# Wider instructions in an attention stage: two heads' maxima and scores per two-bank tile, rows scaled in one instruction, float64 conversion in 28 pieces

## The chip, the cores and the metric

The kernel runs on one NeuronCore of a Trainium2 chip. TensorE (PE) multiplies, VectorE (DVE) and ScalarE (ACT) do elementwise work, GpSimd (POOL) helps, and SyncE (SP) issues nearly all DMAs. The metric is the device time in microseconds (us), and the median of several executions is compared.

## The reference, cut to what matters

Three parts run one after the other; the output of each is the input of the next.

```python
# q, k, v: (4, 12, 448, 64) float32
q_n, k_n = rmsnorm(q, g_q), rmsnorm(k, g_k)
scores = scale * np.matmul(q_n, k_n.transpose(0, 1, 3, 2))
scores = scores - np.max(scores, axis=-1, keepdims=True)
attn = np.exp(scores)
attn = attn / (np.sum(attn, axis=-1, keepdims=True) + 1e-09)
out = np.matmul(attn, v)
# mixture of experts: 1792 tokens, 8 experts of at most 224 tokens, greedy assignment
h = np.maximum(x[mask] @ w1[e], 0.0);  out[mask] = h @ w2[e]
# cos MLP
h = x @ w_in;  return (h * np.cos(h)) @ w_out
```

`w_in` (768x2048) and `w_out` (2048x768) arrive as float64. The kernel reads them as pairs of 32-bit words and turns each number into a float32 high and low half before the last part uses them.

## The kernel before, in words

**The order of work.** No engine's order is written by hand. Each operation is recorded as a step (`Plan.add`, through the helper at line 47, which is why most rows of the profile carry L47), with what it reads and writes. `Plan.run` then places the steps one by one with a fixed cost for each (`Plan.cost`) and a due time worked out backwards from the end; on each engine, the step that can start first goes first, and among those about equally early the one due first. Each engine's instructions are issued in that order, and semaphores do the rest. There are two plans: `attention` (with the first part of the routing and the conversion), then `moe` (routing, experts, MLP). All instructions of the first plan stand ahead of those of the second on each engine.

**Attention** works on 24 pairs of heads (4 batches x 6 pairs). For a pair, `turn` scales the rows and transposes them with PE into `kk` and `qq`. `shifts` finds for every query the maximum of its scores: seven products `s` of 448 columns go one after the other through a ring of two PSUM tiles (`b1`, tile name `s1`, one bank each), and DVE reduces each into a column of `cm`. Three products belong to each head, on 64 of PE's rows, and the seventh is shared. The maxima are transposed, negated by ACT into `cr`, and copied by two small DMAs (`sr<-cr`) into one row. `scores` makes, for each of four blocks of 112 keys, the two heads' scores with eight matmuls of 64 rows each (the last two add the negated maxima from `sr`), into the two PSUM tiles of ring `bs` (`st`), one head in each; ACT takes the exponential of each into a tile `pf`. `weigh` multiplies `pf` with the values (`po`) and sums the rows (`dn`). `rows` and `tail` transpose the result and scale it: DVE writes `xk` in two halves of 256 columns; for the last pair ACT does it in eight pieces.

**Conversion.** `Narrow` works through 56 pieces (32 of `w_in`, three blocks of 128 rows each; 24 of `w_out`, four blocks each; `EARLY = 56` puts all of them into the attention plan). A piece is loaded into `nr` (a ring of four), ACT takes magnitudes into `na`, DVE does two `tensor_scalar`, two `scalar_tensor_tensor` and, after another ACT step, one `tensor_tensor`, and a DMA stores the piece to DRAM. These steps depend on no step of attention; they share its engines. In `moe`, `narrow.plan` is called once more with nothing left to do, and only allocates tiles.

Of the kernel before, what the change touches and what calls it, by code (L numbers as in the profile page):

```python
# [15 lines left out]
I32 = mybir.dt.int32  # L16
AF = mybir.ActivationFunctionType
ALU = mybir.AluOpType
AX = mybir.AxisListType
# [31 lines left out]
class Plan:  # L51
# [96 lines left out]
    def ring(self, pool):  # L148

        def make(name, n, shape, dt=F32):  # L150
            tiles = [pool.tile(shape, dt, name=f"{name}{i}") for i in range(n)]
            at = [0]

            def take():
                at[0] += 1
                return tiles[(at[0] - 1) % n]
            return take
        return make
# [93 lines left out]
class Narrow:  # L252
# [1 line left out]

    WIDE = {"wi": 3, "wo": 4}

    def __init__(self, nc, pairs):

# [11 lines left out]
    def plan(self, plan, pool, last):  # L272

        nc = self.nc
        most = max(self.WIDE.values())
        raw = [pool.tile([128, most, 256], I32, name=f"nr{b}") for b in range(4 - (self.i > 0))]
        mag = [pool.tile([128, most, 128], I32, name=f"na{b}") for b in range(2)]
        v = plan.vector
        for i, (src, dst, name) in enumerate(self.todo[self.i:last]):
            n = dst.shape[1]  # L280
            r, a = raw[i % len(raw)][:, 0:n], mag[i % 2][:, 0:n]
            words, o = r.rearrange("p k (n t) -> p k n t", t=2), r.bitcast(F32R).rearrange("p k (h n) -> p k h n", h=2)
            low, high, f = words[:, :, :, 0], words[:, :, :, 1], a.bitcast(F32)
            plan.add([("SP", 0.46, lambda r=r, src=src: nc.sync.dma_start(r, src))], [], [r], dma=0.36 * n)
            plan.scalar.activation(f, high.bitcast(F32), AF.Abs)
            v.tensor_scalar(f, f, LEAST, MOST, op0=ALU.max, op1=ALU.min)
            v.tensor_scalar(a, a, 3, 0x3FFFFFF8, op0=ALU.logical_shift_left, op1=ALU.bitwise_and)
            v.scalar_tensor_tensor(a, high, -0x40000000, a, op0=ALU.bitwise_and, op1=ALU.bitwise_or)
            v.scalar_tensor_tensor(a, low, 29, a, op0=ALU.logical_shift_right, op1=ALU.bitwise_or)
            plan.scalar.activation(o[:, :, 0], f, AF.Copy)  # L290
            plan.either("tensor_tensor", o[:, :, 1], f, o[:, :, 0].bitcast(F32), op=ALU.subtract)
            plan.add([("SP", 0.46, lambda o=o, dst=dst: nc.sync.dma_start(dst, o.bitcast(F32)))], [o], [name], dma=0.36 * n)
        self.i = last


B, H, S, D = 4, 12, 448, 64
CP, NC = 112, 4
# [4 lines left out]
EPS = 1e-9  # L302
SAME = 4.0
TUNE_A = (3.5, 0.3, 4.5, 0.7, 30.0, 1.2)
NPF = 18
NXE = 6
LAST = 3
COLD = 20
# [3 lines left out]
ACC = ()  # L312
END = 20.0
NKQ = 5
XKA = 0
XKL = 1
QND = False
SSA = 1
# [17 lines left out]
def attention(tc, P, R, ident, q, k, v, g_q, g_k, w_gate, x_dram, L, other):  # L336
# [4 lines left out]
    with ExitStack() as ctx:  # L341
        cst = ctx.enter_context(tc.tile_pool(name="a_cst", bufs=1))
        pp = ctx.enter_context(tc.tile_pool(name="a_ps", bufs=1, space=PSUM))
        ve, sc, pe = P.vector, P.scalar, P.tensor
        ring = P.ring(cst)

        def bank(name, n):
            return P.ring(pp)(name, n, [128, 512])

        keys = [cst.tile([128, 2, S], F32R, name=f"kk{i}") for i in range(NKQ)]  # L350
        queries = [cst.tile([128, 2, S], F32R, name=f"qq{i}") for i in range(NKQ)]
# [5 lines left out]
        ones = cst.tile([CP + 1, 2, 32], F32, name="ones")  # L357
        part = cst.tile([CP, NC, 8, H + 1], F32, name="part")
        raw = ring("qk", 3, [CP, 2, 4, NC * D])
# [6 lines left out]
        mix = [cst.tile([128, 128], F32R, name=f"mx{i}") for i in range(4)]  # L366
        cms = ring("cm", 2, [128, 2 * NC])
        crs = ring("cr", 2, [2 * NC, 128], F32R)
        pfs = ring("pf", NPF, [CP + 1, S])
        xes = ring("xe", NXE, [128, S])  # L370
        dns = ring("dn", 2, [128, CP])
        xks = ring("xk", 2, [CP, NC, 2 * UP * D])
        recs = ring("r", 3, [CP, NC, 2])
        abs_ = ring("ab", 1, [CP, 2, NC, 128], BF16)
        NPR = B * NP
        bt, b1, bs, bo, bd = bank("t", 2), bank("s1", 2), bank("st", 2), bank("po", 1), bank("dn", 1)

        R.on(P, bd)

# [34 lines left out]
        for i, g in enumerate((g_q, g_k)):  # L414
            for z in range(2):
                o = gcol[z * D:(z + 1) * D, i:i + 1]
# [64 lines left out]
        def shifts(P_):  # L481


            cm, x = cms(), 7
            k, q = keys[P_ % NKQ], queries[P_ % NKQ]
            for m in (0, 4, 1, 5, 2, 6, 3):
                p = b1()[:, :S]
                if m == 3:
                    w, y = mix[P_ % 4], k[:, 0]
                else:  # L490
                    h, c = (0, 128 * m) if m < 3 else (1, D + 128 * (m - 4))
                    r = slice(h * D, (h + 1) * D)
                    w, y = q[r, 0, c:c + 128], k[r, 0]
                pe.matmul(p, w, y, start=True, stop=True)
                ve.tensor_reduce(cm[:, m:m + 1], p, AX.X, ALU.max)
            p, cr = bt()[0:x, 0:128], crs()[0:x]
            pe.transpose(p, cm[:, 0:x], ident)
            sc.activation(cr, p, AF.Copy, scale=-1.0)
            t = shift_rows[P_ % 4]
            for h in range(2):  # L500
                copy(t[h * D:h * D + 1].rearrange("o (m p) -> o m p", p=128), cr[3 * h:3 * h + 4])
# [17 lines left out]
        def scores(P_, a, z):  # L519

            k, q, t = keys[P_ % NKQ], queries[P_ % NKQ], shift_rows[P_ % 4]
            for c in range(a, z):
                sl = slice(c * CP, (c + 1) * CP)
                ps = [bs()[0:CP, :S] for h in range(2)]

                def both():
                    for j in range(4):
                        for h in range(2):
                            r = slice(h * D, (h + 1) * D)
                            w = heads[r] if j == 3 else k[r, j == 1, sl]  # L530
                            y = t[r, h * D:h * D + S] if j == 3 else q[r, int(j == 2)]
                            pe.matmul(ps[h], w, y, start=j == 0, stop=j == 3)

                P.halves = True
                block(both)
                P.halves = False
                for h in range(2):
                    pf = exps[P_, h, c] = pfs()
                    sc.activation(pf[0:CP], ps[h], AF.Exp)

        outs = {}

        def weigh(P_):


            po, pd = bo()[:, :S], bd()[:, 0:CP]
            t = vals.pop(P_).rearrange("p h (c d) -> p h c d", d=D)
            P.beside = True
            for c0 in range(0, NC, 2):
                def both():  # L550
                    for c in range(c0, c0 + 2):
                        for h in range(2):
                            pe.matmul(po[h * D:(h + 1) * D], t[:, h, c], exps[P_, h, c][0:CP], start=c == 0,
                                      stop=c == NC - 1)

                block(both)
            sums_of[P_] = pd
            outs[P_] = xes()
            sc.activation(outs[P_], po, AF.Copy)

            def sums():
                for h in range(2):
                    for c in range(NC):
                        n, e = CP + (c == 0), exps.pop((P_, h, c))
                        for j in range(NC):
                            pe.matmul(pd[32 * j:32 * j + 32], ones[0:n, h], e[0:n, j * CP:(j + 1) * CP],
                                      start=h == 0 and c == 0, stop=False)

            block(sums)

            def logits():
                for j in range(NC):
                    pe.matmul(pd[32 * j:32 * j + 32], wg[:, P_ % NP], outs[P_][:, j * CP:(j + 1) * CP], start=False,
                              stop=True)

            block(logits)
            P.beside = False
# [16 lines left out]
        def tail(P_, xk, e, r):  # L594
            xe, p = outs.pop(P_), bt()[0:CP]
            P.begin()
            for c in range(NC):
                pe.transpose(p[:, c * 128:(c + 1) * 128], xe[:, c * CP:(c + 1) * CP], ident)
            P.finish()
            for z in range(2):  # L600
                cs = slice(2 * z, 2 * z + 2)
                o = xk[:, cs, 2 * e * D:2 * (e + 1) * D].rearrange("p c (h d) -> p c h d", h=2)
                i = p.rearrange("p (c h d) -> p c h d", c=NC, h=2)[:, cs]
                if z < XKA or P_ >= NPR - XKL:
                    for c in range(2):
                        for h in range(2):
                            sc.activation(o[:, c, h], i[:, c, h], AF.Copy, scale=r[:, 2 * z + c, h:h + 1])
                else:
                    ve.tensor_tensor(o, i, r[:, cs].unsqueeze(3).to_broadcast([CP, 2, 2, D]), op=ALU.mult)

        roots_of, xk_of = {}, {}

# [80 lines left out]
CP, NCOL, E, CAP = 112, 16, 8, 224  # L693
# [415 lines left out]
def moe(tc, P, R, ident, x_rows, w1, w2, w_in, w_out, out, narrow):  # L1109

    nc = tc.nc
    with ExitStack() as ctx:
# [172 lines left out]
            nc.gpsimd.memset(apart, 0.0)  # L1285

        P.shared = False
        narrow.plan(P, cst, len(narrow.todo))
        behind = None

        def fetch(t, step=None):
# [12 lines left out]
            mlp(grp, lambda: fetch(grp[-1] + 1, behind))  # L1304
        P.run(zip(chain, chain[1:]), *TUNE_B)

EARLY = 56


@with_exitstack  # L1310
# [60 lines left out]
```

## Time and profile before

| | us |
|---|---|
| median of 3 runs | 1221.68 (1220.99 to 1222.58) |
| the profiled execution, its own time | 1224.71 |
| its span, first to last instruction | 1222.9 |
| PE busy in the span | 1142.1 (93%) |
| DVE busy | 852.9 (70%) |
| ACT busy | 657.5 (54%) |
| POOL busy | 150.3 (12%) |
| mean granted clock of TensorE | 0.964 |

PE's busy time includes the modelled ends of pipelined matmuls, so it is not PE at its peak. The shares are means over stages with different limits: the attention stage fills about the first 367 us, the routing of the first expert follows, and experts and MLP take the rest.

### The profile page before, as it was taken

How to read it: one execution, taken by the hardware profiler on the slowest of the kernel's cores; microseconds unless marked ns; L12 is line 12 of the kernel's file. 1: busy time of each engine (PE TensorE's matmuls, PEld its weight loads, DVE VectorE, ACT ScalarE, POOL GpSimd, SP SyncE). 2: the span in 40 equal slices, each digit the busy share in tenths (PEclk: the TensorE clock that was granted, in tenths of full speed). 3: DMA queues.
4: the chain of work that ended last, by engine and by line, in shares of the span. 5: the costliest groups of instructions: out<-in, count | busy, mean ns of one | idle time of the engine just before them, and what ended most of it. 6: DMA issues, size and time to landing. Idle time of an engine off the chain costs nothing.

```text
span 1222.9 us, 23588 instructions
## 1 busy us (share of the span) xinstructions
PE 1142.1 (93%) x8712; PEld 947.5 (77%) x8712; DVE 852.9 (70%) x2335; ACT 657.5 (54%) x1576; POOL 150.3 (12%) x287
## 2 busy tenths in 40 slices
PE   7999999999985989998999999899999899999996
PEld 4555655565543889887899988799988789999996
DVE  6998999999958865794576498277579458546401
ACT  5976877776643533781455384255468155435400
POOL 5532324241000000000001000002000001100001
PEclk8999999999995889999999999899999999899999
DMA  8357666766642656779468767838776856766761
GB/s 203 115 165 226 209 209 189 247 232 219 215 141 63 166 154 205 236 241 245 163 164 241 209 214 251 257 91 228 218 245 233 240 192 162 207 197 211 233 216 60
DMA packets 181395, 241.86 MB, mean 198 GB/s; under 512 B 14176, under 2 KB 156960, under 8 KB 175136
## 3 DMA queue, kind: packets, MB, share of 16 engines
q1 hardware_dynamic: 178720, 229.35, 61.1%
q0 software_dynamic: 2560, 11.01, 3.2%
q8 instruction: 68, 1.11, 0.4%
q14 instruction: 47, 0.39, 0.1%
HBM read 203.71 MB, written 36.52 MB: 196 GB/s over the span
## 4 chain that ended last, share of the span: by engine, by line
PE 50%; DVE 27%; DMA 13%; ACT 6%; issue 3%; POOL 1%; SPq 1%; POOLq 0%; DVEq 0%; ACTq 0%
PE acc L47 35%; DVE r L47 4%; DVE cm L47 4%; PE po L47 3%; PE st L47 3%; DMA xr<-x,idx 3%; DVE na L47 3%; ACT oh L47 3%; DVE oh L47 3%; DMA AB<-rows 3%; PE s L47 2%; PE dn L47 2%; PE tr L47 2%; DVE wx L47 1%; DMA ws<-in_moe_w_dram 1%
## 5 line engine op out<-in xcount | busy, mean ns | idle before, releaser
L47 PE MATMUL acc<-gh,wx 128*128 128x224 f32 (+1 forms) x1952 | 374.9, 317 | 0.0
L47 PEld LDWEIGHTS acc<-gh,wx 128*128 128x128 f32 x1952 | 286.5, 195 | 24.7 <-issue 13.1
L47 PE MATMUL acc<-x2h,wx 128*128 128x448 f32 x768 | 223.6, 369 | 0.0
L47 DVE TENSOR_TENSOR wx<-ws,wx 128x768 fp32r<-128x768 f32 (+1 forms) x112 | 120.0, 1071 | 64.5 <-ACT wx L1191 64.5
L1191 ACT ACTIVATE wx<-ws 128x768 fp32r<-128x768 f32 (+1 forms) x112 | 104.7, 936 | 109.6 <-PE acc L47 69.6
L47 PEld LDWEIGHTS acc<-x2h,wx 128*128 128x128 f32 x768 | 144.6, 188 | 15.5 <-issue 3.1
L47 ACT ACTIVATE oh<-oh 128x896 bf16<-128x896 bf16 x96 | 90.4, 942 | 107.0 <-DVE oh L47 105.5
L47 PE MATMUL acc<-gl,wx 128*128 128x448 f32 (+1 forms) x400 | 146.1, 365 | 0.0
L47 PE MATMUL acc<-x2l,wx 128*128 128x448 f32 x384 | 140.7, 366 | 0.0
L47 PE MATMUL acc<-xe,wx 128*128 128x224 f32 x1152 | 137.1, 280 | 0.6 <-DVE wx L47 0.5
L47 PEld LDWEIGHTS acc<-xe,wx 128*128 128x128 f32 x1152 | 134.4, 196 | 1.3 <-DVE wx L47 0.7
L47 ACT ACTIVATE pf<-st 112x448 f32<-112x448 f32 x192 | 93.4, 537 | 38.7 <-PE st L47 36.5
L47 DVE TENSOR_REDUCE cm<-s 128x1 f32<-128x448 f32 x168 | 99.5, 616 | 5.2 <-PE s L47 3.8
L1152 POOL DMA_INDIRECT xr<-x,idx x16 | 17.7, 1107 | 652.7 <-issue 215.9
L47 DVE TENSOR_SCALAR oh<-AB,b 128x896 bf16<-128x896 f32 x96 | 61.6, 683 | 50.5 <-DMA AB<-rows 34.4
L47 PE MATMUL st<-qq,kk 64*112 64x448 f32 x576 | 92.3, 391 | 2.3 <-ACT pf L47 2.2
L47 ACT ACTIVATE r<-r 128x448 f32<-128x448 f32 x128 | 72.8, 573 | 36.5 <-DVE r L47 35.1
L47 PE MATMUL po<-pf,vr 112*64 112x448 f32 x384 | 84.5, 560 | 0.0
L47 PEld LDWEIGHTS acc<-gl,wx 128*128 128x128 f32 x400 | 77.4, 193 | 5.2
L47 PEld LDWEIGHTS acc<-x2l,wx 128*128 128x128 f32 x384 | 72.2, 188 | 5.8
L47 PEld LDWEIGHTS st<-qq,kk 64*112 64x112 f32 x576 | 49.4, 171 | 25.7 <-ACT pf L47 10.1
L47 DVE SCALAR_TENSOR_TENSOR na<-nr,na 128x384 int32<-128x384 int32 (+1 forms) x112 | 68.0, 632 | 0.5
(237 smaller groups left out, 1662.5 us busy)
## 6 DMA issues: line engine op xcount, KB each, us to landing
wx<-w_in SPq DMA_DIRECT2D x64, 768.0 KB
wx<-w_out SPq DMA_DIRECT2D x48, 1024.0 KB
ws<-in_moe_w_dram SPq DMA_DIRECT2D x64, 384.0 KB
ws<-in_moe_w_dram SPq DMA_DIRECT2D x48, 512.0 KB
nr<-in_moe_w_in_dram SPq DMA_DIRECT2D x32, 384.0 KB
w_in<-nr SPq DMA_DIRECT2D x32, 384.0 KB
nr<-in_moe_w_out_dram SPq DMA_DIRECT2D x24, 512.0 KB
w_out<-nr SPq DMA_DIRECT2D x24, 512.0 KB
```

The source lines that it names most:

```text
L47: self.plan.add([(self.eng, self.plan.cost(self.eng, name, out, r, kw), lambda: f(*args, **kw))], r, w)
L1152: P.add([("POOL", 1.03, lambda x=x, h=h: nc.gpsimd.indirect_dma_start(out=x, out_offset=None, in_=x_rows, in_offset=bass.IndirectOffsetOnA ...
L1191: P.add([("ACT", 0.093 + n * 0.1067, lambda: nc.scalar.activation(hi, s, AF.Copy)), ("DVE", 0.07 + n * 0.0667, lambda: nc.vector.tensor_co ...
```

## The change

Four things are made wider; the arithmetic stays.

1. In `shifts`, the products of head 0 and head 1 for one block of 128 queries go side by side into one PSUM tile of two banks, and one `tensor_reduce` over 896 columns writes two columns of `cm`. The ring `s1` has one such tile in place of two tiles of a bank each. The two matmuls are one step of the plan. The shared seventh product uses the first bank of the same tile.
2. In `scores`, both heads' scores go into one tile of two banks (ring `st` of one), and one exponential over 896 columns writes one `pf` tile of both heads. `NPF` goes from 18 to 9, with tiles twice as wide.
3. In `tail`, one `tensor_tensor` of 512 columns takes the place of two of 256.
4. `Narrow` takes 6 and 8 blocks at a time: 28 pieces, a ring of three `nr` tiles of twice the size, `EARLY = 28`. The empty call in `moe` is gone.

```diff
-    WIDE = {"wi": 3, "wo": 4}
+    WIDE = {"wi": 6, "wo": 8}
...
-        raw = [pool.tile([128, most, 256], I32, name=f"nr{b}") for b in range(4 - (self.i > 0))]
+        raw = [pool.tile([128, most, 256], I32, name=f"nr{b}") for b in range(3)]
...
-NPF = 18
+NPF = 9
...
-        bt, b1, bs, bo, bd = bank("t", 2), bank("s1", 2), bank("st", 2), bank("po", 1), bank("dn", 1)
+        bt, b1, bs, bo, bd = bank("t", 2), bank("s1", 1, 2), bank("st", 1, 2), bank("po", 1), bank("dn", 1)
...
-            for m in (0, 4, 1, 5, 2, 6, 3):
-                p = b1()[:, :S]
-                if m == 3:
-                    w, y = mix[P_ % 4], k[:, 0]
-                else:
-                    h, c = (0, 128 * m) if m < 3 else (1, D + 128 * (m - 4))
-                    r = slice(h * D, (h + 1) * D)
-                    w, y = q[r, 0, c:c + 128], k[r, 0]
-                pe.matmul(p, w, y, start=True, stop=True)
-                ve.tensor_reduce(cm[:, m:m + 1], p, AX.X, ALU.max)
+            for m in range(3):
+                p = b1()[:, :, :S]
+
+                def both():
+                    for h in range(2):
+                        r = slice(h * D, (h + 1) * D)
+                        c = 128 * m + h * D
+                        pe.matmul(p[:, h], q[r, 0, c:c + 128], k[r, 0], start=True, stop=True)
+
+                P.halves = True
+                P.begin()
+                both()
+                P.finish()
+                P.halves = False
+                ve.tensor_reduce(cm[:, m:m + 5:4], p, AX.X, ALU.max)
+            p = b1()[:, 0, :S]
+            pe.matmul(p, mix[P_ % 4], k[:, 0], start=True, stop=True)
+            ve.tensor_reduce(cm[:, 3:4], p, AX.X, ALU.max)
...
-                ps = [bs()[0:CP, :S] for h in range(2)]
+                ps = bs()[0:CP, :, :S]
...
-                            pe.matmul(ps[h], w, y, start=j == 0, stop=j == 3)
+                            pe.matmul(ps[:, h], w, y, start=j == 0, stop=j == 3)
...
-                for h in range(2):
-                    pf = exps[P_, h, c] = pfs()
-                    sc.activation(pf[0:CP], ps[h], AF.Exp)
+                pf = exps[P_, c] = pfs()
+                sc.activation(pf[0:CP], ps, AF.Exp)
...
-            for z in range(2):
-                cs = slice(2 * z, 2 * z + 2)
...
-                    ve.tensor_tensor(o, i, r[:, cs].unsqueeze(3).to_broadcast([CP, 2, 2, D]), op=ALU.mult)
+                ve.tensor_tensor(o, i, r.unsqueeze(3).to_broadcast([CP, NC, 2, D]), op=ALU.mult)
...
-        narrow.plan(P, cst, len(narrow.todo))
...
-EARLY = 56
+EARLY = 28
```

## Rows read from the trace of the kernel before

**Rows 1.** Busy time of each engine by stretch (instructions in brackets), PEclk, DMA, GB/s.
```profile
0.00:60.00 60.00, 50.62 (x313) 31.62 (x314) 48.93 (x150) 42.46 (x176) 32.92 (x99) 0.91 0.63 161
60.00:345.00 285.00, 269.28 (x3010) 159.65 (x3007) 270.58 (x674) 203.09 (x601) 79.35 (x139) 0.99 0.66 213
345.00:372.00 27.00, 20.30 (x235) 10.89 (x232) 11.91 (x58) 12.06 (x31) 0.00 (x0) 0.92 0.27 101
372.00:1223.00 851.00, 801.86 (x5160) 745.31 (x5160) 521.51 (x1457) 399.92 (x771) 38.05 (x50) 0.96 0.66 198
```

**Rows 2.** The same view, the first minute and a later one of the long stretch.
```profile
60.00:120.00 60.00, 55.09 (x636) 32.86 (x635) 52.57 (x131) 41.60 (x142) 19.36 (x34) 0.97 0.60 191
...
240.00:300.00 60.00, 56.11 (x630) 33.44 (x632) 59.29 (x147) 40.23 (x103) 19.49 (x29) 1.00 0.69 230
```

**Rows 3.** Groups of VectorE instructions, 60 to 345 us: busy us, mean ns | idle before.
```profile
L47 DVE TENSOR_REDUCE cm<-s 128x1 f32<-128x448 f32 x140 | 82.6, 615 | 2.7 <-PE s L47 1.7 <-PE st L47 0.2
L47 DVE SCALAR_TENSOR_TENSOR na<-nr,na 128x384 int32<-128x384 int32 (+1 forms) x104 | 62.3, 626 | 0.4
L47 DVE TENSOR_SCALAR na<-na 128x384 int32<-128x384 int32 (+3 forms) x103 | 39.6, 400 | 2.9 <-ACT na L47 2.6
L47 DVE TENSOR_TENSOR nr<-na,nr 128x384 fp32r<-128x384 f32 (+1 forms) x52 | 34.8, 680 | 2.0 <-ACT nr L47 1.8
L47 DVE TENSOR_TENSOR xk<-t,r 112x256 f32<-112x256 f32 x44 | 17.2, 414 | 0.0
```

**Rows 4.** Timeline, VectorE: runs back to back, and one alone (start us, us).
```profile
212.22 0.24 DVE L47 TENSOR_SCALAR t<-K 112x4 int32<-112x4 int32 x2
212.43 0.17 DVE L47 TENSOR_SCALAR W<-t 112x4 f32<-112x4 int32 x1
...
327.35 0.68 DVE L47 SCALAR_TENSOR_TENSOR na<-nr,na 128x512 int32<-128x512 int32 x1
327.95 1.15 DVE L47 TENSOR_REDUCE cm<-s 128x1 f32<-128x448 f32 x2
...
338.23 2.49 DVE L47 SCALAR_TENSOR_TENSOR na<-nr,na 128x512 int32<-128x512 int32 x4
...
342.33 0.74 DVE L47 TENSOR_TENSOR xk<-t,r 112x256 f32<-112x256 f32 x2
```

**Rows 5.** Waits by engine, 60 to 345 us: total us, times, longest us.
```profile
PEld s L47 <- DVE cm L47: 15.5, 25, 1.2
...
PE s L47 <- DVE cm L47: 9.8, 21, 0.9
...
PEld st L47 <- ACT pf L47: 5.8, 16, 1.2
```

**Rows 6.** Timeline, end of stage: scores and exponentials in turn, the last conversion step.
```profile
347.32 1.29 PE L47 MATMUL st<-qq,kk 64*112 64x448 f32 x6 [0.31 <-ACT pf L47]
348.27 0.56 PE L47 MATMUL st<-sr,heads 64*112 64x448 f32 x2
...
348.67 0.98 ACT L47 ACTIVATE pf<-st 112x448 f32<-112x448 f32 x2 [0.96 <-PE st L47]
...
349.26 1.29 PE L47 MATMUL st<-qq,kk 64*112 64x448 f32 x6 [0.44 <-ACT pf L47]
...
350.20 0.69 DVE L47 TENSOR_TENSOR nr<-na,nr 128x512 fp32r<-128x512 f32 x1 [1.02 <-ACT nr L47]
...
350.62 0.98 ACT L47 ACTIVATE pf<-st 112x448 f32<-112x448 f32 x2 [0.46 <-PE st L47]
```

**Rows 7.** Timeline: one maximum, the next product in the freed tile.
```profile
334.52 0.62 DVE L47 TENSOR_REDUCE cm<-s 128x1 f32<-128x448 f32 x1
...
335.19 0.47 PE L47 MATMUL s<-kk,qq 64*128 64x448 f32 x1
```

**Rows 8.** Groups of ScalarE instructions, 60 to 345 us: busy us, mean ns | idle before.
```profile
L47 ACT ACTIVATE pf<-st 112x448 f32<-112x448 f32 x164 | 79.6, 537 | 32.3 <-PE st L47 30.3 <-PE s L47 1.5
```

**Rows 9.** Waits of SyncE's own queue, 0 to 370 us: total us, times, longest us.
```profile
SPq L284 <- DMA w_in<-nr: 49.0, 24, 4.6
SPq L284 <- DMA w_out<-nr: 25.7, 15, 4.2
```

More of the change, by code (lines that the diff above doesn't have):

```diff
@@ L314 @@
 NKQ = 5
-XKA = 0
 XKL = 1
@@ L345, in attention, with bank @@
         ring = P.ring(cst)
-        def bank(name, n):
-            return P.ring(pp)(name, n, [128, 512])
+        def bank(name, n, wide=1):
+            return P.ring(pp)(name, n, [128, 512] if wide == 1 else [128, wide, 512])
         keys = [cst.tile([128, 2, S], F32R, name=f"kk{i}") for i in range(NKQ)]
@@ L368, in attention @@
         crs = ring("cr", 2, [2 * NC, 128], F32R)
-        pfs = ring("pf", NPF, [CP + 1, S])
+        pfs = ring("pf", NPF, [CP + 1, 2, S])
         xes = ring("xe", NXE, [128, S])
@@ L552, in both @@
                         for h in range(2):
-                            pe.matmul(po[h * D:(h + 1) * D], t[:, h, c], exps[P_, h, c][0:CP], start=c == 0,
+                            pe.matmul(po[h * D:(h + 1) * D], t[:, h, c], exps[P_, c][0:CP, h], start=c == 0,
                                       stop=c == NC - 1)
@@ L563, in sums @@
                     for c in range(NC):
-                        n, e = CP + (c == 0), exps.pop((P_, h, c))
+                        n, e = CP + (c == 0), exps[P_, c]
                         for j in range(NC):
-                            pe.matmul(pd[32 * j:32 * j + 32], ones[0:n, h], e[0:n, j * CP:(j + 1) * CP],
+                            pe.matmul(pd[32 * j:32 * j + 32], ones[0:n, h], e[0:n, h, j * CP:(j + 1) * CP],
                                       start=h == 0 and c == 0, stop=False)
@@ L599, in tail @@
             P.finish()
-            for z in range(2):
-                cs = slice(2 * z, 2 * z + 2)
[L602 to L608, printed above, removed]
-                    ve.tensor_tensor(o, i, r[:, cs].unsqueeze(3).to_broadcast([CP, 2, 2, D]), op=ALU.mult)
+            o = xk[:, :, 2 * e * D:2 * (e + 1) * D].rearrange("p c (h d) -> p c h d", h=2)
+            i = p.rearrange("p (c h d) -> p c h d", c=NC, h=2)
+            if P_ >= NPR - XKL:
+                for c in range(NC):
+                    for h in range(2):
+                        sc.activation(o[:, c, h], i[:, c, h], AF.Copy, scale=r[:, c, h:h + 1])
+            else:
+                ve.tensor_tensor(o, i, r.unsqueeze(3).to_broadcast([CP, NC, 2, D]), op=ALU.mult)
         roots_of, xk_of = {}, {}
```

## The prediction

> **What bounds the kernel now.** I read the busy shares by stretch first, because the page's shares mix stages. The change touches only what runs in the first 367 us; from 372 us on nothing of it runs, so those 851 us [rows 1] should stay. Inside the attention stage the reader is to look at which engine has no holes. From 60 to 345 us DVE is busy 270.6 of 285 us, 95%, and in a later minute 59.3 of 60 [rows 1, 2]. PE shows 269.3 of 285 [rows 1], but its ends are modelled, so I ask the waits instead: 25.3 us of the stretch PE or its weight loads sat until DVE had finished a maximum (15.5 and 9.8), and 5.8 us until an exponential was done [rows 5]. An engine that waits for DVE that much is not the one that holds the stage back. The groups turn it round: before the 140 maxima DVE sat idle 2.7 us in all, 1.7 of them for a product [rows 3]. ACT is busy 203 of 285 us and its exponentials wait 30.3 us for PE [rows 1, 8]. So DVE sets the pace from 60 to 345 us, and roughly the last 20 us are another regime: DVE falls to 11.9 of 27 us, the last conversion step starts at 350.20, and PE and ACT hand the scores to and fro [rows 1, 6].
>
> Conversion counts in this. It depends on nothing in attention, but takes the same DVE in the same stretch: 62.3 + 39.6 + 34.8 = 136.7 us of the 270.6 [rows 3]. Whatever DVE saves in any of its groups is therefore time of the stage, as long as DVE always has something ready.
>
> **The change part by part.** *Fewer, wider DVE instructions.* The elements stay; what goes is the fixed cost of an instruction. In a saturated stretch that is what an instruction adds from start to start, not its duration, since durations overlap. Four `scalar_tensor_tensor` of 512 columns take 2.49 us and one alone 0.68: (2.49 - 0.68) / 3 = 0.603 a step. Two maxima of 448 take 1.15, one 0.615: a step of 0.535. Two scalings of 256 take 0.74, one 0.414: 0.326 [rows 3, 4]. The line through 256 and 512 columns has 0.277 / 256 = 1.08 ns a column and leaves 0.05 us at nothing. From the other side, an instruction of 4 columns steps by 0.24 - 0.17 = 0.07 us [rows 4]. The fixed cost lies between 0.05 and 0.07; I take 0.065, nearer the tiny instruction, which consists of little else, because the line's points are rounded to 0.01.
>
> How many go: between 60 and 345 us the 140 maxima are 20 pairs of heads, three instructions saved in each, 60; the 44 scalings become 22, 22 saved; the conversion has 104 + 103 + 52 = 259, half saved, 130 [rows 3]. Together 212 x 0.065 = 13.8 us, with bounds 212 x 0.05 = 10.6 and 212 x 0.07 = 14.8. Instructions saved before 60 us count nothing: that is the startup, DVE is busy only 48.9 of 60 us there [rows 1], and the first pair's serial chain sets it.
>
> The Trainium skill, "Perfetto Trace Analysis", section Optimizing Scalar/DVE Operations, gives a DVE fixed cost of about 60 ns on SBUF and about 125 ns on PSUM. The maxima and scalings read PSUM, and here they step like the others (0.535 for 448 columns), so the trace agrees on SBUF and not on PSUM. By the page the sum would be 82 x 0.125 + 130 x 0.06 = 18.1 us, an estimate; it is a rival below.
>
> *One two-bank tile for the maxima.* Before, a product could be made in one tile while DVE reduced the other. Now DVE must finish 896 columns, PE must see it (0.05 us: a maximum ends at 335.14, the next product starts at 335.19), the product takes 0.47, and only then can the next maximum start [rows 7]: a hole of about 0.57 us, three in each of 23 pairs, 39 us if nothing fills them. What fills them is the rest of DVE's work, 270.6 - 82.6 = 188 us of the stretch [rows 1, 3], nine microseconds for each pair, of which conversion is most; a wide conversion step lasts longer than one hole. The planner knows of the single tile and orders for it, with its own costs. I therefore cost it at what such drift costs now, once more: DVE waits for products 1.7 us [rows 3], so 1.7 us lost. Below: nothing, if the fill is perfect; above: all 39.
> The Trainium skill speaks against this edit: "Perfetto Trace Analysis", section Matmuls, wants independent matmul groups to rotate through different PSUM banks so that evacuation and the next matmuls overlap. Taken by itself it makes the holes above real; whether they are filled is what the trace of after must say.
>
> On PE the two products of a block now stand together and on different halves of the rows. That saves PE time, costed at nothing because PE is not the bound; if it were, it would be a gain.
>
> *One exponential of 896 columns.* Two take 0.98 us [rows 6]; a wide one ends sooner by one fixed cost of ACT, for which I have no row and take 0 to 0.07, as on DVE. ACT has a quarter of the stretch free [rows 1], so this is worth nothing there. At the end of the stage it isn't: scores and exponentials alternate with a period of 350.62 - 348.67 = 1.95 us. Before, the first exponential starts at 348.67, while the two last matmuls end at 348.27 + 0.56 = 348.83; and the first head's next scores start at 349.26, while the exponentials end at 348.67 + 0.98 = 349.65 [rows 6]. Both overlaps (0.16 and 0.39) go; but the second head's matmuls run beside the first's, so the 0.39 was mostly no use, and the shorter exponential gives back a little. I take +0.15 us a block (bounds 0 and 0.4) for the eight blocks of the last two pairs, which run after conversion has ended: 1.2 us lost. In the middle of the stage the same 0.15 on the 16 waits of `st` for `pf` [rows 5] falls on PE, hidden by DVE's load.
>
> *Conversion in 28 pieces.* Same bytes, half the DMAs, each twice as long. The load of a piece already waits in SP's queue for an earlier store, 49.0 + 25.7 us in all, 4.6 at the longest [rows 9]; behind it stand the small `sr<-cr` copies, which the scores need. Waits for `sr` don't appear in the list of PE's waits, so there is cover; if it is gone, a wait of 4.6 us that becomes 9 would be paid by PE. Cost: nothing, upper bound below. DVE's longer steps hold up maxima a little longer; PE has room for that.
>
> **Sum.** 13.8 - 1.7 - 1.2 = 10.9 us gained. The profiled execution took 1224.71 us (span 1222.9) and becomes 1213.8; it stood 3.0 us above the median of the runs, 1221.7, so the forecast on the median is 1221.7 - 10.9 = 1210.8, say 1211. Its own range: 10.6 - 1.7 - 3.2 (0.4 a block) = 5.7 to 14.8 saved, 1207 to 1216.
>
> **The rivals.**
> *The single tile stalls DVE* (slower). If the planner's order and the chip drift apart, the holes stay open. Beside 13.8 - 1.2 = 12.6 us gained, the change is worth nothing when 12.6 / 39, a third of the holes, stay open; at 60% it loses 23.4 - 12.6 = 11 us: 1232. For it: PE's 25.3 us of waits for maxima show that the order already drifts with two tiles [rows 5]. Against it: DVE itself waited only 1.7 us, and there are 188 us of other work. Chance 0.15.
> *Larger transfers block SP's queue.* One pair in three pays 3 of the extra 4.6 us: 8 x 3 = 24 us on PE, of which the waits for DVE that PE has anyway cover perhaps half; 12 lost against 10.9 gained: 1223, no change. For it: the waits in [rows 9]. Against: no wait of PE for `sr`. Chance 0.09.
> *The bound moves.* If PE's modelled ends are its real load, it has 285 - 269.3 = 15.7 us to give, 5.8 of which go on waiting for exponentials [rows 1, 5]: at most 9.9. If a last wide conversion piece (136.7 us for 52 pieces, so 2 x 2.6 = 5.3) is left over for the end, where now DVE is half free, 4.6 remain: 1217. For it: PE's busy share; against it: its waits for DVE. Chance 0.12.
> *The fixed cost on PSUM is larger than the steps say.* If a maximum's whole excess over its columns counts, 0.615 - 448 x 0.00108 = 0.13 us, the 82 PSUM merges give 10.7 and the rest 8.5: 19.2 - 2.9 = 16.3, 1205. It needs DVE to run apart from its next instruction, which the overlaps in [rows 4] deny. Chance 0.08.
> By the page's figures this rival would give 18.1 - 2.9 = 15.2 us, 1206 to 1207.
>
> **How the numbers follow.** The forecast has 0.56. With it, the larger gain (0.08) and the moved bound (0.12), the change is faster by over 0.2% (2.4 us, about what a measurement can tell from no change): 0.76, less 0.03 for a bound that moves at once: 0.73. No change: those 0.03 and the queue's 0.09, so 0.12. Slower: 0.15. The range goes from 1204 (the larger gain) to 1223 (the blocked queue) and leaves out the stall and a little of the larger gain.
>
> **What the profile after would show.** `cm` 72 instructions of 896 columns near 1.08 us and 24 near 0.615; wide `na` of 768 and 1024 near 1.0 and 1.2; `pf` 96 near 0.91. DVE still above 93% in the long stretch, the last store of `xk` near 356 instead of 367, and the time behind the attention unchanged within a microsecond. If DVE shows holes that end with `PE s`, the single tile was mis-costed; if PE waits for `sr<-cr`, the transfers; if DVE falls below 90% with neither, the bound has moved.

## The result and the profile after

The changed kernel takes 1232.4 us in the median (1231.9 to 1236.8) against 1222.1 us: a ratio of 1.0092, interval 1.0066 to 1.0117. It is slower, where 11 us of gain were forecast. The profiled execution took 1236.8 us with a span of 1235.0; that of before 1224.7 and 1222.9; both are a little slower than the other executions of their kernel in this comparison.

Where the time went is seen by stretch. Of after, in the view of [rows 1], with the long stretch also cut in two, and the whole cut where the attention ends:

```profile
60.00:345.00 285.00, 261.98 (x2936) 152.38 (x2935) 246.04 (x450) 197.82 (x498) 82.36 (x148) 0.98 0.62 204
...
60.00:240.00 180.00, 163.77 (x1822) 95.10 (x1819) 144.76 (x273) 132.43 (x405) 61.52 (x112) 0.97 0.58 181
240.00:345.00 105.00, 98.20 (x1116) 57.28 (x1116) 101.28 (x178) 65.40 (x95) 20.85 (x36) 0.98 0.70 244
...
0.00:380.80 380.80, 335.15 (x3546) 194.68 (x3546) 309.13 (x612) 249.38 (x650) 109.67 (x228) 0.96 0.60 190
380.80:1235.00 854.20, 801.01 (x5166) 743.68 (x5166) 525.49 (x1490) 400.36 (x775) 38.04 (x50) 0.96 0.65 198
```

Of before, the same cuts, the last two at the end of the attention:

```profile
60.00:240.00 180.00, 170.75 (x1909) 101.14 (x1906) 167.03 (x421) 134.90 (x439) 58.70 (x107) 0.99 0.66 206
240.00:345.00 105.00, 98.53 (x1103) 58.52 (x1101) 103.55 (x254) 68.19 (x162) 20.65 (x33) 1.00 0.68 225
...
0.00:366.70 366.70, 338.79 (x3546) 201.43 (x3546) 327.13 (x848) 256.37 (x802) 112.27 (x237) 0.98 0.63 198
366.70:1222.90 856.20, 803.26 (x5166) 746.05 (x5166) 525.80 (x1489) 401.15 (x774) 38.05 (x50) 0.96 0.66 198
```

The cuts at 366.7 and 380.8 are where the last scaled rows `xk` are ready. The attention ends 14.1 us later; what follows takes 854.2 instead of 856.2 us, so nothing was lost there. DVE's work did shrink: 309.1 us busy in the attention in place of 327.1, with 612 instructions instead of 848. But from 60 to 240 us DVE is busy only 144.8 of 180 us, where it was 167.0. The saved work became idle time, and more than that; from 240 us on DVE is nearly full again (101.3 of 105 us), and the stage ends late. Over the whole attention DVE's work fell by 18.0 us while its idle time rose from 366.7 - 327.1 = 39.6 to 380.8 - 309.1 = 71.7 us, by 32.1: together the 14.1 us.

All of it is lost by the time that the last copy of maxima (`sr<-cr`) starts. These copies, of after and of before (count, duration in ns, first and last start in us):

```profile
L389 SPq DMA_DIRECT2D sr<-cr x48: 572/579/942, 22.4 to 359.9; - x48
...
L390 SPq DMA_DIRECT2D sr<-cr x48: 572/579/1058, 24.0 to 345.1; - x48
```

The last one starts 14.8 us later, and from there to the end of the attention it is 20.9 us where it was 21.6.

The wide instructions cost what was expected: a maximum of 896 columns 1.08 us and an exponential of 896 columns 0.92 (forecast near 1.08 and 0.91; the middle number is the median in ns):

```profile
L47 DVE TENSOR_REDUCE cm<-s x96: 607/1083/1095, 15.5 to 354.7; 128x2 f32<-128x896 f32 x72, 128x1 f32<-128x448 f32 x24
...
L47 ACT ACTIVATE pf<-st x96: 890/917/922, 31.7 to 374.3; 112x896 f32<-112x896 f32 x96
```

DVE's groups of after, as in [rows 3]:

```profile
L47 DVE TENSOR_REDUCE cm<-s 128x2 f32<-128x896 f32 (+1 forms) x79 | 76.5, 968 | 11.8 <-PE s L47 11.3
L47 DVE SCALAR_TENSOR_TENSOR na<-nr,na 128x768 int32<-128x768 int32 (+1 forms) x50 | 54.1, 1090 | 0.2
...
L47 DVE TENSOR_REDUCE ss<-sq 112x8 f32<-112x512 f32 x15 | 10.2, 681 | 8.3 <-ACT sq L47 8.3
```

and the last of these groups in before:

```profile
L47 DVE TENSOR_REDUCE ss<-sq 112x8 f32<-112x512 f32 x13 | 8.8, 677 | 0.0
```

The idle time before the maxima rose from 2.7 to 11.8 us, and before the sums of squares 8.3 us appeared. PE's waits on ACT rose too, by the waits of after:

```profile
PEld st L47 <- ACT pf L47: 19.5, 28, 2.7
...
PE st L47 <- ACT pf L47: 10.5, 17, 2.5
...
PEld s L47 <- DVE cm L47: 2.1, 3, 1.2
...
PE s L47 <- DVE cm L47: 1.5, 3, 0.8
```

Compared with [rows 5], the waits have changed sides: PE hardly waits for DVE's maxima any more (2.1 and 1.5 us in place of 15.5 and 9.8); it waits for exponentials (19.5 in place of 5.8). A first reading was theory A: the maxima are a serial chain through one tile, and the scores stand at its end. The small copies of the maxima seem to say so in SP's queue, where they (line 389) are the longest wait of after:

```profile
SPq L389 <- ACT sq L47: 70.9, 9, 17.6
...
SPq L389 <- ACT cr L47: 38.1, 11, 11.2
```

The experiments show that this reading was too quick.

### The profile page after: what moved, and what is told of

Read it like the earlier page. It is cut to its first block, busy times and chain, and to the rows that moved or that the text cites. A ratio compares the mean times of both kernels' runs of the same rounds, so it can differ in the third digit from the quotient of the medians.

```text
span 1235.0 us, 22982 instructions
## 1 busy us (share of the span) xinstructions
PE 1136.2 (92%) x8712; PEld 938.4 (76%) x8712; DVE 834.6 (68%) x2100; ACT 649.7 (53%) x1424; POOL 147.7 (12%) x278
## 4 chain that ended last, share of the span: by engine, by line
PE 43%; DVE 22%; DMA 14%; ACT 8%; issue 2%; POOL 1%; SPq 0%; POOLq 0%; DVEq 0%; ACTq 0%
PE acc L47 34%; DVE r L47 4%; DMA xr<-x,idx 3%; DMA AB<-rows 3%; DVE na L47 3%; ACT oh L47 3%; DVE oh L47 3%; PE st L47 3%; PE po L47 2%; DMA qk<-in_k_dram 2%; DMA ws<-in_moe_w_dram 2%; PE tr L47 2%; DVE cm L47 2%; DVE wx L47 1%; DMA wx<-w_in 1%
## 5 line engine op out<-in xcount | busy, mean ns | idle before, releaser
L47 ACT ACTIVATE pf<-st 112x896 f32<-112x896 f32 x96 | 87.6, 913 | 49.9 <-PE st L47 48.9
L47 DVE TENSOR_REDUCE cm<-s 128x2 f32<-128x896 f32 x96 | 93.1, 969 | 20.9 <-PE s L47 20.4
L47 PE MATMUL st<-qq,kk 64*112 64x448 f32 x576 | 85.1, 401 | 16.8 <-ACT pf L47 15.8
L47 PE MATMUL po<-pf,vr 112*64 112x448 f32 x384 | 90.2, 591 | 0.1
L47 PEld LDWEIGHTS st<-qq,kk 64*112 64x112 f32 x576 | 44.2, 176 | 43.4 <-ACT pf L47 26.6
L47 ACT ACTIVATE sq<-qk 112x64 f32<-112x64 f32 (+1 forms) x195 | 57.5, 301 | 25.8 <-DMA qk<-in_k_dram 14.5
```

Of the source, the lines that this page charges most:

```text
L47: self.plan.add([(self.eng, self.plan.cost(self.eng, name, out, r, kw), lambda: f(*args, **kw))], r, w)
```

## The experiments

Five theories were tried. A: the maxima's chain through the single tile ends too late. B: the wide conversion steps hold up DVE's other work. C: the single tile of scores costs the overlap of PE and ACT. D: any edit of the steps gives the planner another order, and the order of the kernel before is worth several us. E: conversion is due later, because its ring turns 28/3 times where it turned 56/4 times, and is left to the end.

| run | ratio to before | 95% interval | attention ends (us) |
|---|---|---|---|
| maxima alone | 1.0100 | 1.0061 to 1.0140 | 376.6 |
| conversion alone | 1.0065 | 1.0043 to 1.0088 | 376.7 |
| scores alone | 1.0045 | 1.0020 to 1.0070 | 374.8 |
| scaling alone | 1.0050 | 1.0029 to 1.0071 | 374.0 |
| all but the maxima | 1.0039 | 1.0004 to 1.0074 | 378.4 |
| all but the conversion | 1.0092 | 1.0060 to 1.0124 | 379.0 |
| all but the scores | 1.0235 | 1.0168 to 1.0302 | 387.9 |
| before, another order (1) | 1.0035 | 1.0010 to 1.0060 | 378.5 |
| before, another order (2) | 1.0062 | 1.0035 to 1.0088 | 375.4 |
| scaling, old order | 1.0006 | 0.9981 to 1.0032 | 367.0 |
| scores, old order | 0.9999 | 0.9979 to 1.0019 | 366.5 |
| after, maxima due early | 1.0010 | 0.9984 to 1.0035 | 367.5 |
| after, conversion due early | 1.0011 | 0.9978 to 1.0045 | 366.6 |
| after, both due early (4, 4) | 1.0000 | 0.9966 to 1.0033 | 363.8 |
| before, maxima due early | 1.0096 | 1.0059 to 1.0133 | 379.7 |
| after, due 4 and 8 | 0.9883 | 0.9861 to 0.9904 | 352.1 |
| after, due 5 and 4 | 0.9980 | 0.9955 to 1.0004 | 355.8 |
| after, due 5 and 8 | 0.9966 | 0.9942 to 0.9990 | 363.8 |

Each ratio has its own runs of the kernel before beside it, whose medians lie between 1217.8 and 1222.1 us; so kernels are compared by their ratios. The last column is from one profiled execution each, and not always a typical one: for all but the maxima and for the first other order it was the slowest of ten (1235.0 and 1232.0 us), for the maxima alone the fastest of four (1226.8).

**One part at a time.** Each part of the diff was put into the kernel before by itself, here the scaling:

```diff
-            for z in range(2):
...
-                    ve.tensor_tensor(o, i, r[:, cs].unsqueeze(3).to_broadcast([CP, 2, 2, D]), op=ALU.mult)
+                ve.tensor_tensor(o, i, r.unsqueeze(3).to_broadcast([CP, NC, 2, D]), op=ALU.mult)
```

> The kernel before with the maxima alone changed: two products in one two-bank tile, one maximum of 896 columns, one such tile. Theory A (the maxima of a pair become a serial chain through one tile, each round lengthened by whatever DVE takes in between, and the scores wait for its end): 4 to 12 us slower than before. Theory B (the wide conversion steps hold up DVE's other work): 0 to 4 us faster, since 72 fixed costs of 0.065 us are saved. Theory C (the single tile of scores): the same as B.

> The kernel before with the conversion alone in 28 pieces. Theory A: between 8 us faster (130 fixed costs saved) and the same. Theory B: 5 to 12 us slower. Theory C: as A.

> The kernel before with the scores alone changed: both heads in one two-bank tile, one exponential of 896 columns. Theories A and B: within 2 us of before. Theory C (scores and exponentials lose their overlap, 0.15 to 0.4 us in each of 96 blocks): 5 to 12 us slower.

> The kernel before with the scaling of rows alone in one instruction of 512 columns. All theories: 0 to 1.5 us faster (23 fixed costs of 0.065 us). A change of 3 us or more either way would say that a new order of the steps by itself moves the time by as much as the effects looked for (theory D).

All four are slower. The maxima, the conversion and the scores lose about what theories A, B and C each foretold for its own part, so these three runs don't tell the theories apart. The scaling does: it takes 23 instructions away and merges no tiles, and is slower by 0.5%, with its attention ending 7 us late. That is theory D's mark. The four ratios add up to 2.6%, and together they gave 0.9%: parts measured this way don't add.

**One part left out.** Three more kernels are the changed one with the lines of before for one part, as here for the scores:

```diff
-                ps = bs()[0:CP, :, :S]
+                ps = [bs()[0:CP, :S] for h in range(2)]
...
-                pf = exps[P_, c] = pfs()
-                sc.activation(pf[0:CP], ps, AF.Exp)
+                for h in range(2):
+                    pf = exps[P_, h, c] = pfs()
+                    sc.activation(pf[0:CP], ps[h], AF.Exp)
```

> The changed kernel with the maxima as before (seven products through two tiles of one bank, seven maxima of 448 columns). Theory A: the loss is gone, 1212 to 1222 us. Theory B (wide conversion steps) or C (single tile of scores): it stays above 1228.

> The changed kernel with the conversion in 56 pieces as before. Theory A: rounds of the maxima get shorter by the shorter steps between them, but stay serial: 1224 to 1232 us. Theory B: the loss is gone, at or below 1222. Theory C: 1228 or more.

> The changed kernel with the scores as before (two tiles of one bank, two exponentials). Theories A and B: it stays at 1228 to 1234 us. Theory C: at or below 1222.

No part carries the whole loss. Without the wide maxima 0.39% of the 0.92% is left, 1223.4 us, between what theory A foretold (1212 to 1222) and what B and C did (above 1228). Without the wide conversion all of it is left, as A and C foretold. The kernel that keeps the old scores is much worse, against all theories. And the waits don't follow the tile alone. DVE's wait for products, 60 to 240 us, in the kernel with two tiles (all but the maxima):

```profile
DVE cm L47 <- PE s L47: 15.7, 10, 3.1
```

and in the kernel with only the single tile (maxima alone):

```profile
DVE cm L47 <- PE s L47: 3.2, 9, 0.8
```

These are single executions, one slow and one fast for its kernel; but the kernel with leads 4 and 8 below, profiled near its median, has the single tile too and waits 2.0 us. The single tile by itself doesn't make the holes: in some orders they are filled. In the form in which the prediction priced it, a hole for each wide maximum, theory A falls.

**The order by itself.** Two kernels have every instruction of before and one constant of the planner changed:

```diff
-TUNE_A = (3.5, 0.3, 4.5, 0.7, 30.0, 1.2)
+TUNE_A = (3.5, 0.33, 4.5, 0.7, 30.0, 1.2)
```

in the first, and 4.7 for 4.5 in the second.

> The kernel before, no instruction changed; the planner's allowance for crossing engines is 0.33 in place of 0.3, so the same instructions are issued in another order. Theory D (the order of the kernel before is worth several us, and any edit of the steps loses it): 3 to 9 us slower than before, with the attention ending 5 us or more later. Theories A to C: within 2 us.

> The kernel before, no instruction changed; the planner's lead for transfers is 4.7 in place of 4.5. Theory D: 3 to 9 us slower. Theories A to C: within 2 us.

Both are slower, by 0.35% and 0.62%, and in the profiled executions, both slow ones for their kernels, the attention ends 9 to 12 us later. In the first, DVE loses from 60 to 240 us nearly 10 us of work with no instruction changed; in the second only 2, so an order can lose its time elsewhere too. The first and the second:

```profile
60.00:240.00 180.00, 166.49 (x1792) 98.17 (x1791) 157.35 (x404) 129.32 (x440) 52.69 (x106) 0.95 0.61 189
...
60.00:240.00 180.00, 169.62 (x1920) 103.10 (x1918) 165.15 (x433) 136.53 (x466) 54.39 (x101) 1.00 0.66 206
```

TensorE's clock doesn't sort the kernels by itself. It is granted at 2.4 or 1.2 GHz, and from 60 to 345 us its mean, as a share of the upper level, was 0.99 in the kernel before and 0.98 in the changed one; but it was 0.99 too with the maxima alone, whose attention ends 10 us late:

```profile
60.00:345.00 285.00, 259.01 (x2885) 149.85 (x2875) 264.08 (x597) 202.10 (x597) 76.40 (x139) 0.99 0.67 215
```

**Wide instructions in the old order.** Here the planner still counts the two narrow steps; the first issues nothing, the second the wide instruction:

```diff
-                    ve.tensor_tensor(o, i, r[:, cs].unsqueeze(3).to_broadcast([CP, 2, 2, D]), op=ALU.mult)
+                    f = (lambda: nc.vector.tensor_tensor(oa, ia, ra, op=ALU.mult)) if z else (lambda: None)
+                    P.add([("DVE", P.cost("DVE", "tensor_tensor", o, [i, rb], {}), f)], [i, rb], [o])
```

(`oa`, `ia`, `ra` are the operands of all 512 columns); the exponential is done likewise.

> The scaling in one instruction of 512 columns, alone, in the order of the kernel before: the planner still counts two steps, the first issues nothing and the second issues the wide instruction. Theory D: 0 to 2 us faster than before. If the wide instruction itself were the loss seen when the scaling was changed alone: 4 us or more slower.

> The two-bank tile of scores and the exponential of 896 columns, alone, in the order of the kernel before, by the same means. Theory D: within 2 us of before. Theory C (lost overlap of scores and exponentials): 4 us or more slower.

The traces show that the order was held: apart from the merged instructions, ACT starts its work on the same tiles in the same sequence as in the kernel before. Both are level with before, and the attention ends at 367.0 and 366.5 us instead of 366.7. So the 0.5% of each part alone was the order, and the lost overlap of scores and exponentials (theory C) costs nothing that shows; losses or gains of up to some 3 us would not show in these runs. The maxima and the conversion can't be had in the old order in this way, since their steps depend on one another differently; that was not tried.

**Due times.** The planner adds a lead to each transfer when it works due times out backwards. The next kernels give single transfers more of it; instructions and tiles are those of the changed kernel.

```diff
-            d += lag if s.dma is not None else 0.0
+            d += lag + s.lead if s.dma is not None else 0.0
...
+            P.lead = 4.0
             for h in range(2):
                 copy(t[h * D:h * D + 1].rearrange("o (m p) -> o m p", p=128), cr[3 * h:3 * h + 4])
+            P.lead = 0.0
...
+        P.lead = 6.0
         other(P, cst)
+        P.lead = 0.0
```

Each step keeps the lead that is set when it is recorded. The hunk with 4.0 is for the copies of the maxima, the one with 6.0 for the conversion's loads and stores; the first two runs have one of them each, the third has both with 4.0, and the fourth is the kernel before with the first.

> The changed kernel; the copies of the maxima (sr<-cr) get 4 us more lead in the planner's due times, so the maxima are begun earlier. Instructions and tiles unchanged. Theory A (the serial chain of maxima through one tile ends too late for the scores): 4 to 9 us faster than the changed kernel, 1224 to 1228. Theory E (conversion, whose ring turns 28/3 times where it turned 56/4, is due later and is left to the end): the same as the changed kernel within 3 us. Theory D (only the order): anything within 5 us.

> The changed kernel; the conversion's transfers get 6 us more lead in the due times, which makes up for the fewer turns of its ring. Theory E: 4 to 9 us faster than the changed kernel. Theory A: the same within 3 us. Theory D: anything within 5 us.

> The changed kernel with 4 us more lead for the copies of the maxima and for the conversion's transfers. If A and E both hold: 1216 to 1224 us, 8 us or more below the changed kernel. If the wide instructions are worth what the prediction summed once the order suits them: 1210 to 1214.

> The kernel before with the same 4 us more lead for the copies of the maxima. Theory A: no gain, since with two tiles the maxima are in time: the same or slower by up to 9 us. If a longer lead helps any kernel: faster by 4 us or more, and the run on the changed kernel says nothing of the single tile.

Either lead brings the changed kernel back to before, 10 us or so by the ratios, and both together no further that the runs could tell. The lead for the maxima makes the kernel before slower by 1%, some 12 us, where theory A allowed for 9. A and E each foretold that the other's lead would do nothing, and D that either would move less than 5 us; so none of the three is shown to be the cause as it was put. What is shown is that the loss can be undone without touching an instruction, a tile or a transfer. With three other pairs of leads:

> The changed kernel; 4 us more lead for the copies of the maxima, 8 us for the conversion's transfers. If only the order kept the saved fixed costs from showing: 1208 to 1215 us, with the attention ending before 360. If another limit holds the stage (the serial rounds of maxima, scores and exponentials in turn, PE): 1217 to 1224, as with 4 and 4.

> The same with 5 and 4 us. As for 4 and 8: 1210 to 1217 if only the order was in the way, 1217 to 1224 if another limit holds.

> The same with 5 and 8 us. As for 5 and 4. A spread of over 6 us among the three would say that the order decides more than any sum of instruction costs.

With 4 and 8 the kernel takes 1202.9 us where the kernel before took 1217.8, 1.2% less, and by the ratios 2.1% less than the changed kernel. DVE and PE by stretch in it:

```profile
60.00:240.00 180.00, 171.48 (x1964) 101.15 (x1964) 173.77 (x334) 146.11 (x415) 64.11 (x118) 1.00 0.74 239
240.00:345.00 105.00, 98.65 (x1127) 57.40 (x1128) 82.59 (x155) 58.82 (x85) 20.78 (x32) 1.00 0.49 170
...
0.00:352.10 352.10, 323.79 (x3546) 192.63 (x3546) 304.68 (x613) 247.99 (x650) 113.09 (x228) 0.99 0.66 206
```

From 60 to 240 us DVE is busy 173.8 of 180, and its wait for the single tile has shrunk to 2.0 us:

```profile
DVE cm L47 <- PE s L47: 2.0, 6, 0.7
```

Conversion now runs ahead. The stores of its last part, in SP's rows (count, duration in ns, first and last start), of the changed kernel

```profile
L292 SPq DMA_DIRECT2D w_out<-nr x12: 326/344/1567, 261.7 to 366.1; - x12
```

and of this one

```profile
L294 SPq DMA_DIRECT2D w_out<-nr x12: 332/344/396, 196.0 to 322.8; - x12
```

The other two orders of the same instructions come to 0.9980, which is not clear of 1, and 0.9966. Over 12 us lie between the medians of the three.

## Why the prediction was wrong

*The bound.* The rows bear it out for the kernel before (DVE idle 14.4 of the 285 us), and no run tests it by itself. It doesn't hold to the end in the best order found: with leads 4 and 8 DVE works only 82.6 of 105 us from 240 to 345 us, PE 98.7 (its ends are modelled). There the bound has moved.

*The fixed cost.* Right. A step of the conversion of 768 columns, three back to back in that kernel and one alone in the changed one:

```profile
169.60 2.69 DVE L47 SCALAR_TENSOR_TENSOR na<-nr,na 128x768 int32<-128x768 int32 x3
...
198.79 0.95 DVE L47 SCALAR_TENSOR_TENSOR na<-nr,na 128x768 int32<-128x768 int32 x1
```

The step is (2.69 - 0.95) / 2 = 0.87; with 0.603 at 512 columns [rows 4] that is 1.04 ns a column and 0.07 us fixed, the upper end of the bounds. The maxima read PSUM and show the same: 1.083 us for 896 columns and 0.615 for 448 are 1.04 ns a column, and a step of 0.535 [rows 4] leaves 0.07 us. The larger cost on PSUM that the Trainium skill gives ("Perfetto Trace Analysis", section Optimizing Scalar/DVE Operations) is not seen here, and the rival built on such a cost falls.

*The sum.* That the kernel with leads 4 and 8 gains 14 us, and the sum of the fixed costs was 13.8, is a coincidence as far as the runs go. It is the best of three orders that differ by 12 us; its DVE is idle for 352.1 - 304.7 = 47.4 us of the attention, where before it was 39.6. In the held order the scaling saves 1.5 us by the sum, too little for that run to show. So that a fixed cost saved on DVE is time of the stage in an unchanged order is not shown.

*The failing step* is the condition "as long as DVE always has something ready". The prediction stated it, and let nothing in the sum depend on it but 1.7 us for the single tile. In the changed kernel DVE's idle time from 60 to 240 us went from 13.0 to 35.2 us (180 less its busy time), which alone is more than the whole gain, and in the whole attention it rose by 32.1 us. The prediction took "the planner knows of the single tile and orders for it" as a reason for a small loss. The runs show that the planner's order is itself a term, which the sum put at nothing: unchanged instructions lose 0.35% and 0.62% by it, changed ones move between 0.988 and 1.009.

*The slower rival* gave the right figure, 1232 us, for a reason that holds at most in part; that it hit the number is luck. Its sign is there: from 60 to 345 us DVE is busy 246.0 of 285 us, 86%, with holes that end with a product, 11.3 us against 1.7. But DVE's idle time in that stretch rose by 24.5 us, so these holes are 9.6 of it. And they come and go with the order, in kernels with two tiles (15.7 us) as with one (3.2 and 2.0). Its price was also a little high: the rows it names give 0.05 + 0.47 = 0.52 us for a hole and not 0.57. The rule of the Trainium skill that it was set beside ("Perfetto Trace Analysis", section Matmuls), to rotate PSUM banks so that emptying one overlaps the next matmuls, agrees with PE's turn to waiting for exponentials, 19.5 us in place of 5.8; as a cost it isn't seen in the scores in the old order, 0.9999.

*The exponential.* It was expected to lose 1.2 us at the stage's end. The run in the old order shows neither that nor its absence, since its interval is 0.2%, 2.4 us, either way. One of 896 columns takes 0.92 us where two took 0.98.

*The queue and the bound's move.* The scores did wait for copies of the maxima in the changed kernel, 9.4 us in four waits, where before there were none:

```profile
its engine sat idle before it (us, times) until:
  DMA sr<-cr: 9.4, 4
```

The queue as the prediction meant it is not seen to be the reason. Loads that wait for an earlier store of the conversion do reach 8.4 us, near the 9 it named, but add up to 38.5 us instead of 74.7 [rows 9]:

```profile
SPq L284 <- DMA w_in<-nr: 20.0, 8, 5.4
SPq L284 <- DMA w_out<-nr: 18.5, 5, 8.4
```

And the conversion ended 15 us later than before (its last store starts at 366.1 instead of 350.9), more than the left-over piece of 5.3 us that the rival of the moving bound feared. With leads 4 and 8 it ends early, at 322.8. Whether either delay is a cause of the late end or only goes with it is not shown.

*Open:* which of the two late chains, the maxima or the conversion, started the loss in the changed kernel, since curing either cured it; and what makes the order of the kernel before so much better than its neighbours. Nor was the kernel before given as many orders as the changed one, so how its best would stand against 1202.9 us is not known.

## What to carry to other kernels

Where a program orders instructions by due times, an edit that removes or merges steps changes the whole order, and the new order can cost more than the edit saves: hold the order fixed to learn what the instruction is worth, and vary the order with the instructions fixed to learn what the order is worth, before believing a run of one part. When pieces grow and rings shrink, look at what that does to their due times. A saturated engine makes saved work into saved time only while something is always ready for it, so the idle time of that engine by stretch is the first thing to read after.

## What was not expected

The same instructions on the same tiles ran between 0.9883 and 1.0092 of the kernel before by order alone, 2.1% apart. And executions of a single kernel spread further than the first few of the kernel before let expect (1221.0 to 1223.5 us): all but the maxima gave 1219.9 to 1235.0 us in ten, and the kernel before itself 1210.6 to 1227.6 in 29 later ones. Part of it can lie behind the attention, where the instructions are the same: 856.2 us in the profiled execution of before, 849.5 in that with leads 4 and 8.
